# Neighbouring value blocks of a sparse-attention tile: copied on chip from the preceding tile's buffer instead of loaded

## The chip, the cores and the metric

The kernel runs on one core of a Trainium2 chip. The core has a matrix engine (PE, with its weight loads as PEld), a vector engine (DVE), a scalar engine (ACT), a general engine (Pool, or GpSimd), and SP, which issues most of the DMA transfers. SBUF, the on-chip memory, has 128 partitions; PSUM, in banks, takes what PE writes. Each engine works through its own queue in order and waits on semaphores for the others.

The metric is the device time of one execution in microseconds. The profile and the trace come from one execution taken by the hardware profiler; times inside it count from the span's start.

## The reference: what is computed

Block-sparse attention, then a mixture of experts that sends every token to one expert. Cut to what matters:

```python
B, H, S, D = 4, 8, 768, 64      # block = 32, so 24 blocks of 32 rows
scores = q @ k^T / sqrt(D)
mask = |blk_i - blk_j| <= 1                                  # the row's own block and its two neighbours
mask |= blk_i == 0 or blk_j == 0 or blk_i == 23 or blk_j == 23   # first and last block: dense
mask |= three sampled blocks per row block
attn = softmax(where(mask, scores, -1e9)) @ v
x = attn as (3072 tokens, 512)
e = argmax(x @ w_gate + modality_bias[modality_id])
out = gate * (relu(x @ w1[e]) @ w2[e])                       # 8 experts, 512 -> 1024 -> 512
```

The change touches only the values `v` that the sparse rows of the attention read.

## The kernel before

**Tiles.** The batch is cut into two halves of two sequences (`half`). In a half, the first and last row block are dense work (items `"d"`), and the other 22 row blocks are taken in pairs: tile `m` (0 to 10) holds row blocks `i = 2m+1` and `i+1`. There are 22 such sparse tiles, numbered `g = 11 * half + m`. Each row block (`n` = 0 or 1) attends to eight blocks: four that both row blocks of the tile share (`i`, the first block, the last block, `i+1`) and four of its own (one outer neighbour, `i-1` or `i+2`, and three sampled).

**Value buffers.** Two buffers `vbuf` are used in turn, by `g % 2`. Each has 128 partitions and three columns of 1024 values (two sequences of 512). A block takes 32 partitions of one column:

| partitions | column 0 (own blocks of `n` = 0) | column 1 (shared) | column 2 (own blocks of `n` = 1) |
|---|---|---|---|
| 0 to 31 | sampled | block `i` | block `i+2` |
| 32 to 63 | sampled | first block | sampled |
| 64 to 95 | sampled | last block | sampled |
| 96 to 127 | block `i-1` | block `i+1` | sampled |

`fetch_v` (line 472) fills the fixed places: the first and last block once per buffer and half (line 478, only for `m < 2`), `i` and `i+2` by one load (line 479), `i-1` and `i+1` by another (line 480). `fetch_own` (line 484) loads the six sampled blocks, whose numbers are read into registers on SP, by six loads (line 492). `weigh_shared` (L551) multiplies column 1, `weigh_own` (L560) columns 0 and 2. Keys have buffers of their own, `kbuf`, which Pool fills from dense keys already on chip (`share_k`, L454, L458 and, for the sampled blocks, L469).

**Order.** The order of the instructions on each engine is written out by hand. The work is a list of items (a dense pair of heads, or one row block of one sequence of a sparse tile, so four items a sparse tile). A loop over ticks `t` runs each stage of the items with a lag in ticks after the item's own number (`LAG`, line 60): scores S 0, maximum M 1, exponential X 2, transposes T and copies A 4, the shared product W 5, the own product V 7, the division O 8. Inside a tick the stages come in the order `OTSMGVXAYW`, and side work is hooked between them at places 0 to 7. For the first 14 ticks the order is the token list `START` (line 50).

Side work is placed by ticks relative to `last(g)`, the number of the last item of tile `g`: the key sharing of tile `g` no earlier than three ticks before its first item (`QP`), `fetch_v` at `last(g-2) + 8`, place 2 (`VL`), which is right after the own product of the tile that used the buffer, and the two halves of `fetch_own` at `last(g-2) + 8` and `+ 10` (`VG`). SP issues all of these in order, with the loads of queries (L141), dense keys and values (L153, L159), the rows written to `x_d` (L322) and, towards the end of the attention, the first weights of the experts (L680, L684). At most a few DMA issues stand open at once; a further issue waits on SP.

Towards the end of the attention the first two expert groups are begun early (`early_groups`, one step a tick at place 2): weights are loaded, cast by ACT (L688) and split into a high and a low part by DVE or, for some pieces (`POOL_SPLITS`), by Pool (L689).

Of the kernel before, what the change touches and what calls it, by code (L numbers as in the profile page):

```python
# [15 lines left out]
ALU = mybir.AluOpType  # L16
# [4 lines left out]
P = 128  # L21
# [18 lines left out]
NM = NB // 2 - 1  # L40
# [12 lines left out]
O01 W02 tb tb T10 A03 tb X11 S13 A10 qp0 tb tb tb tb tb tb O02 M13 tb tb T11 tb tb  # L53
X12 kl1 S0000 S0001 A11 X13 tb h8 tb W03 T12 tb O03 M0000 tb M0001 W10 h9 tb A12 tb tb tb T13
A13 O10 tb qp1 S0010 X0000 W11 tb h10 M0010 X0001 tb vl0 v00 v10 X0010 S0011 S0100 tb tb h11 T0000 h12 tb
A0000 M0011 T0001 tb S0101 A0001 M0100 W12 W13 O11 v11 O12 O13 vl1 h13 X0011 v01
""".split()
START_TICKS = 14
DENSE_AFTER = (22, 38, 43, 45)
# [8 lines left out]
KL = (0, 3)  # L68
QP = (-3, 7)
VL = (8, 2)  # L70
VG = ((8, 4), (10, 6))

DENSE_IN = ((28, 32, 16, 24), (53, 53, 38, 46))
# [14 lines left out]
def attention_moe(ctx, tc, kD, qD, qH, v0, v1, blocks, modality, w_gate, bias, w1, w2, out):  # L88
    nc = tc.nc
# [27 lines left out]
    with ExitStack() as actx:  # L117
# [9 lines left out]
        def slot(n, dt=F32):  # L127
            return big.tile([P, 3 * 1024 + 2], dt, name="slot", tag=f"slot{n}", bufs=1)
# [7 lines left out]
        vbuf = [slot(7 + n)[:, 0:3072].rearrange("p (c f) -> p c f", c=3) for n in range(2)]  # L136
# [313 lines left out]
        def share_k(m, half):  # L450
            i, g = 2 * m + 1, half * NM + m
            kg = kbuf[g % 2]
            if m:
                nc.gpsimd.tensor_scalar(kg[:, 3:5, :], kbuf[(g - 1) % 2][:, 7:9, :], 1.0, 1.0, ALU.mult, ALU.mult)  # L454

            def put(slots, blocks):
                for b in range(HB):
                    nc.gpsimd.tensor_scalar(kg[:, slots, b * P:(b + 1) * P].rearrange("p s (c f) -> p c s f", c=2), kd[half * HB + b][:, :, blocks, :], 1.0, 1.0, ALU.mult, ALU.mult)  # L458

            if m < 2:  # L460
                put(slice(5, 7), slice(0, NB, NB - 1))
            if m == 0:
                put(slice(3, 5), slice(i - 1, i + 1))
            put(slice(7, 9), slice(i + 1, i + 3))
            _, regs = nc.values_load_multi_w_load_instructions(
                rb_i[0:1, 3 * i:3 * i + 6], [ET.Pool], min_val=0, max_val=NB - 1, skip_runtime_bounds_check_because=NO_CHECK)
            for k, reg in enumerate(regs):
                for b in range(HB):
                    nc.gpsimd.tensor_copy(kg[:, k + k // 3 * 6, b * P:(b + 1) * P].rearrange("p (c f) -> p c f", c=2), kd[half * HB + b][:, :, bass.ds(reg, 1), :].rearrange("p c j f -> p c (j f)"))  # L469


        def fetch_v(m, half):
            i, g = 2 * m + 1, half * NM + m
            vg = vbuf[g % 2]
            vrow = vH[half].rearrange("(j s) b f -> s j (b f)", s=BLK)
            if m < 2:
                for n, j in ((0, 0), (1, NB - 1)):
                    nc.sync.dma_start(vg[32 + 32 * n:64 + 32 * n, 1, :], vrow[:, j, :])
            nc.sync.dma_start(vg[0:32, 1:3, :], vrow[:, i:i + 3:2, :])
            nc.sync.dma_start(vg[96:P, 0:2, :], vrow[:, i - 1:i + 2:2, :])  # L480

        own = {}

        def fetch_own(m, half, n):
            i, g = 2 * m + 1, half * NM + m
            vg = vbuf[g % 2]
            vrow = vH[half].rearrange("(j s) b f -> s j (b f)", s=BLK)
            if g not in own:
                own[g] = nc.values_load_multi_w_load_instructions(
                    rb_i[0:1, 3 * i:3 * i + 6], [ET.SP], min_val=0, max_val=NB - 1, skip_runtime_bounds_check_because=NO_CHECK)[1]  # L490
            for k, reg in enumerate(own[g][3 * n:3 * n + 3]):
                nc.sync.dma_start(vg[32 * (k + n):32 * (k + n) + 32, 2 * n, :], vrow[:, bass.ds(reg, 1), :].rearrange("p j f -> p (j f)"))
# [612 lines left out]
        for k, it in enumerate(sparse[0] + sparse[1]):  # L1105
            items.append(it)
            if k in DENSE_AFTER:
                c = 2 * DENSE_AFTER.index(k)
# [5 lines left out]
        def side(t, f, place=7):  # L1114
            work_at.setdefault((t, place), []).append(f)
# [31 lines left out]
        def q_load(m, half):  # L1147
            qraw[m, half] = fetch_q(half, m)
# [7 lines left out]
        loads = {"blk": block_ids}  # L1156
        last = lambda g: at["s", g // NM, g % NM, 1, 1]
        for g in range(2 * NM):
            half, m = divmod(g, NM)
            t = at["s", half, m, 0, 0]  # L1160
            kl = lambda m=m, half=half: q_load(m, half)
            qp = lambda m=m, half=half: share_k(m, half)
            vl = lambda m=m, half=half: fetch_v(m, half)
            vg = [lambda m=m, half=half, n=n: fetch_own(m, half, n) for n in range(2)]
            if g < 2:
                loads.update({f"kl{g}": kl, f"qp{g}": qp, f"vl{g}": vl, **{f"v{n}{g}": vg[n] for n in range(2)}})
                continue
            kt = last(g - 2) + KL[0]
            pt = max(kt, t + QP[0])
            vt = last(g - 2) + VL[0]  # L1170
            side(kt, kl, KL[1])
            side(pt, qp, QP[1])
            side(vt, vl, VL[1])
            for n in range(2):
                side(last(g - 2) + VG[n][0], vg[n], VG[n][1])

# [162 lines left out]
```

## Time and profile before

| what | value |
|---|---|
| time, median of 3 runs | 562.62 us (561.59, 562.62, 565.06) |
| the profiled execution's own time | 561.07 us |
| its span in the trace | 559.4 us |
| mean granted PE clock | 0.983 of full speed |
| DMA bytes | 124.68 MB, 223 GB/s over the span |
| loads of 256 KB into value buffers and other slots, `slot<-v` | 44 |
| loads of 128 KB, `slot<-v` | 140 |

The span starts with loads and constants; the sparse tiles run from about 27 to 251 us, and the experts from there to 549 us, followed by the last writes.

How to read the lines: a row of the timeline has its start in microseconds, its length, the engine, the source line, the operation, the tiles as output<-input, the shape (partitions x elements), the count, and in brackets how long the engine stood idle before it and what ended that. `<-issue` means that the engine waited for nothing that the profile shows. A row of groups has the count, the busy time in microseconds, the mean of one in nanoseconds, and the idle time before it. A row of waits says who waited for whom: total, times, longest. A row of stretches has the stretch, its length, the busy time of PE, PEld, DVE, ACT and Pool with counts, the granted clock, the share of the DMA engines that was busy, and GB/s. A piece of the chain has start, length, engine and line. A row of one source line has minimum, median and maximum in nanoseconds.

### The profile page before, as it was taken

How to read it: one execution, taken by the hardware profiler on the slowest of the kernel's cores; microseconds unless marked ns; L12 is line 12 of the kernel's file. 1: busy time of each engine (PE TensorE's matmuls, PEld its weight loads, DVE VectorE, ACT ScalarE, POOL GpSimd, SP SyncE). 2: the span in 40 equal slices, each digit the busy share in tenths (PEclk: the TensorE clock that was granted, in tenths of full speed). 3: DMA queues.
4: the chain of work that ended last, by engine and by line, in shares of the span. 5: the costliest groups of instructions: out<-in, count | busy, mean ns of one | idle time of the engine just before them, and what ended most of it. 6: DMA issues, size and time to landing. Idle time of an engine off the chain costs nothing.

```text
span 559.4 us, 18870 instructions
## 1 busy us (share of the span) xinstructions
PE 519.3 (93%) x7274; PEld 434.7 (78%) x7274; DVE 368.9 (66%) x1151; ACT 327.1 (58%) x746; POOL 180.2 (32%) x413
## 2 busy tenths in 40 slices
PE   7799888899999996989999999999999999999992
PEld 5477656667776774779888898989989899898972
DVE  4796666677687885985986456655566555665560
ACT  3679755776777874762564545545455454554560
POOL 1746524533354553403134330320303213032130
PEclk9999998999999997999999999999999999999997
DMA  7885999797977789977567875757667567675730
GB/s 288 291 245 151 258 237 256 209 247 234 234 148 214 211 219 262 253 200 264 190 244 242 322 242 192 263 187 240 236 199 260 189 223 243 206 259 185 237 111 22
DMA packets 48691, 124.68 MB, mean 223 GB/s; under 512 B 7376, under 2 KB 7504, under 8 KB 48592
## 3 DMA queue, kind: packets, MB, share of 16 engines
q1 hardware_dynamic: 44512, 110.26, 65.9%
q0 software_dynamic: 4080, 13.12, 6.6%
q8 instruction: 59, 0.97, 0.7%
q14 instruction: 40, 0.33, 0.2%
HBM read 110.76 MB, written 12.86 MB: 221 GB/s over the span
## 4 chain that ended last, share of the span: by engine, by line
PE 76%; DMA 10%; DVE 4%; issue 4%; ACT 2%; SPq 1%; POOL 1%; POOLq 0%; ACTq 0%; DVEq 0%
PE bank L504 8%; PE bank L729 8%; PE bank L712 7%; PE bank L728 7%; PE bank L727 7%; PE bank L714 7%; PE bank L713 7%; PE bank L529 7%; DMA slot<-v 6%; PE bank L551 3%; PE bank L560 3%; PE bank L577 2%; DMA slot<-w 2%; DMA x_d<-xr 2%; PE bank L701 2%
## 5 line engine op out<-in xcount | busy, mean ns | idle before, releaser
L689 DVE TENSOR_TENSOR slot<-slot 128x1024 fp32r<-128x1024 f32 x96 | 120.2, 1257 | 100.6 <-ACT slot L688 95.9
L688 ACT CAST slot<-slot 128x1024 fp32r<-128x1024 f32 x104 | 108.0, 1049 | 107.0 <-PE bank L729 46.6
L712 PE MATMUL bank<-slot 128*128 128x256 f32 x384 | 108.4, 282 | 0.0
L714 PE MATMUL bank<-slot 128*128 128x256 f32 x384 | 107.7, 281 | 0.0
L713 PE MATMUL bank<-slot 128*128 128x256 f32 x384 | 107.6, 280 | 0.0
L520 ACT ACTIVATE a<-y,mn 128x256 f32<-128x256 f32 x176 | 87.9, 506 | 6.7 <-DVE mn L512 6.2
L729 PE MATMUL bank<-slot 128*128 128x512 f32 x200 | 79.2, 396 | 1.1 <-DVE slot L720 1.1
L738 POOL DMA_INDIRECT out<-slot,si x21 | 21.2, 1009 | 182.4 <-ACT slot L734 179.4
L727 PE MATMUL bank<-slot 128*128 128x512 f32 x200 | 80.0, 400 | 0.0
L728 PE MATMUL bank<-slot 128*128 128x512 f32 x200 | 79.0, 395 | 0.0
L469 POOL COPY slot<-slot 128x128 f32 x264 | 64.6, 297 | 27.6 <-issue 27.5
L712 PEld LDWEIGHTS bank<-slot 128*128 128x128 f32 x384 | 72.2, 188 | 0.6
L713 PEld LDWEIGHTS bank<-slot 128*128 128x128 f32 x384 | 72.2, 188 | 0.4
L714 PEld LDWEIGHTS bank<-slot 128*128 128x128 f32 x384 | 72.2, 188 | 0.0
L512 DVE CUSTOM_DVE_ANT_1 y<-bank,smask 128x256 f32<-128x256 f32 x176 | 66.1, 417 | 1.9 <-PE bank L504 1.6
L529 PE MATMUL bank<-ident,a 128*128 128x128 f32 x352 | 55.1, 286 | 7.2 <-DVE mn L512 5.4
L534 ACT COPY at<-bank 128x512 f32<-128x512 f32 x66 | 38.0, 577 | 29.4 <-PE bank L529 28.8
L504 PE MATMUL bank<-slot,q_raw 64*32 64x256 f32 x1408 | 52.4, 393 | 1.6 <-DVE mn L512 1.0
L529 PEld LDWEIGHTS bank<-ident,a 128*128 128x128 f32 x352 | 39.0, 144 | 14.0 <-DVE mn L512 5.0
L729 PEld LDWEIGHTS bank<-slot 128*128 128x128 f32 x200 | 37.6, 188 | 11.0 <-DVE slot L720 2.0
L728 PEld LDWEIGHTS bank<-slot 128*128 128x128 f32 x200 | 37.6, 188 | 8.1 <-DVE slot L689 0.4
L727 PEld LDWEIGHTS bank<-slot 128*128 128x128 f32 x200 | 37.6, 188 | 7.8 <-ACT slot L887 0.3
(290 smaller groups left out, 804.0 us busy)
## 6 DMA issues: line engine op xcount, KB each, us to landing
slot<-w SPq DMA_DIRECT2D x105, 512.0 KB
slot<-v SPq DMA_DIRECT2D x140, 128.0 KB
slot<-v SPq DMA_DIRECT2D x44, 256.0 KB
slot<-v SPq DMA_DIRECT2D x8, 768.0 KB
x_d<-xr SPq DMA_DIRECT2D x22, 256.5 KB
q_raw<-qH SPq DMA_DIRECT2D x22, 256.0 KB
slot<-kD SPq DMA_DIRECT2D x7, 768.0 KB
x_d<-xrd SPq DMA_DIRECT2D x2, 256.5 KB
```

The source lines that it names most:

```text
L504: nc.tensor.matmul(sp[u][32 * pr:32 * pr + 32, b * 256:(b + 1) * 256], lhsT=q[r, b * NPAIR + pr, n, :], rhs=kv[r, s0:s0 + 8, b, pr, :], st ...
L512: nc.vector.tensor_tensor_reduce(y[:, u, :].rearrange("p (s f) -> p s f", s=8), sp[u][:, b * 256:(b + 1) * 256].rearrange("p (s f) -> p s ...
L520: nc.scalar.activation(a[:, u, :], y[:, u, :], AF.Exp, bias=mn[:, u:u + 1], scale=-1.0, accum_out=total[:, u:u + 1])
L529: nc.tensor.transpose(tp[:, k:k + P], a[:, u, c * P:(c + 1) * P], ident)
L688: nc.scalar.copy(h, staged(n))
L689: (eng or (nc.gpsimd if n in POOL_SPLITS else nc.vector)).tensor_tensor(l, staged(n), h.bitcast(F32), ALU.subtract)
L712: nc.tensor.matmul(o, lhsT=h[:, fs], rhs=xh[g % 2][:, c, :], start=c == 0 and f % 2 == 0, stop=False)
L713: nc.tensor.matmul(o, lhsT=h[:, fs], rhs=xl[g % 2][:, c, :], start=False, stop=False)
L714: nc.tensor.matmul(o, lhsT=l[:, fs], rhs=xh[g % 2][:, c, :], start=False, stop=c == 3 and f % 2 == 1)
L727: nc.tensor.matmul(o, lhsT=hh[0][:, f, ts_], rhs=h[:, fs], start=f == 0, stop=False)
L728: nc.tensor.matmul(o, lhsT=hh[0][:, f, ts_], rhs=l[:, fs], start=False, stop=False)
L729: nc.tensor.matmul(o, lhsT=hl[f // 4][:, f % 4, ts_], rhs=h[:, fs], start=False, stop=f == 7)
```

## The change

For every tile but the first of a half, two of the four blocks that `fetch_v` loaded are no longer loaded. Block `i-1` of tile `m` is block `i+1` of tile `m-1`, and block `i` of tile `m` is block `i+2` of tile `m-1`; both lie in the other buffer, in the same partitions, one column to the right. Pool copies them with two operations of 32 partitions by 1024 elements (`share_v`). The two loads stay, with one block each. The first tile of a half loads all four as before.

The copies of tile `g` are placed at `last(g-2) + 11`, place 2 (`VS`), three ticks after the tile's loads; those of tile 1 are a token of `START`. They read the buffer of tile `g-1` and write the buffer that tile `g-2` has left. So they must follow the own product of tile `g-2` and the loads of tile `g-1`; the shared product of tile `g`, and the loads of tile `g+1` into the places that were read, must follow them.

```diff
-A0000 M0011 T0001 tb S0101 A0001 M0100 W12 W13 O11 v11 O12 O13 vl1 h13 X0011 v01
+A0000 M0011 T0001 tb S0101 A0001 M0100 W12 W13 O11 v11 O12 O13 vl1 vs1 h13 X0011 v01
...
 VL = (8, 2)
+VS = (11, 2)
...
-            nc.sync.dma_start(vg[0:32, 1:3, :], vrow[:, i:i + 3:2, :])
-            nc.sync.dma_start(vg[96:P, 0:2, :], vrow[:, i - 1:i + 2:2, :])
+            if m == 0:
+                nc.sync.dma_start(vg[0:32, 1:3, :], vrow[:, i:i + 3:2, :])
+                nc.sync.dma_start(vg[96:P, 0:2, :], vrow[:, i - 1:i + 2:2, :])
+                return
+            nc.sync.dma_start(vg[0:32, 2, :], vrow[:, i + 2, :])
+            nc.sync.dma_start(vg[96:P, 1, :], vrow[:, i + 1, :])
+
+
+        def share_v(m, half):
+            g = half * NM + m
+            new, old = vbuf[g % 2], vbuf[(g - 1) % 2]
+            for r, c in ((slice(96, P), 0), (slice(0, 32), 1)):
+                nc.gpsimd.tensor_scalar(new[r, c, :], old[r, c + 1, :], 1.0, 1.0, ALU.mult, ALU.mult)
...
             side(vt, vl, VL[1])
+            if m:
+                side(last(g - 2) + VS[0], lambda m=m, half=half: share_v(m, half), VS[1])
```

More of the change, by code (lines that the diff above doesn't have):

```diff
@@ L1165, in attention_moe @@
             if g < 2:
-                loads.update({f"kl{g}": kl, f"qp{g}": qp, f"vl{g}": vl, **{f"v{n}{g}": vg[n] for n in range(2)}})
+                loads.update({f"kl{g}": kl, f"qp{g}": qp, f"vl{g}": vl, "vs1": lambda: share_v(1, 0), **{f"v{n}{g}": vg[n] for n in range(2)}})
                 continue
```

## The prediction

> **What bounds the kernel now.** I read the page first: busy shares, the slices, and the chain that ended last.
>
> ```profile
> PE 519.3 (93%) x7274; PEld 434.7 (78%) x7274; DVE 368.9 (66%) x1151; ACT 327.1 (58%) x746; POOL 180.2 (32%) x413
> PEclk9999998999999997999999999999999999999997
> DMA  7885999797977789977567875757667567675730
> PE 76%; DMA 10%; DVE 4%; issue 4%; ACT 2%; SPq 1%; POOL 1%; POOLq 0%; ACTq 0%; DVEq 0%
> ```
>
> TensorE (PE) is busy for 93% of the span and carries 76% of the chain. DMA carries 10%, and its busiest slices lie in the first half, which is the attention. So the next view is the busy time by stretch: all of the steady attention, its last part, and the experts.
>
> ```profile
> core 0: us, PE busy (x) PEld busy (x) DVE busy (x) ACT busy (x) POOL busy (x), PEclk, DMA share, GB/s
> 40.00:251.00 211.00, 190.56 (x4790) 145.69 (x4790) 154.30 (x761) 151.55 (x485) 92.00 (x295) 0.97 0.87 224
> 206.00:250.00 44.00, 36.28 (x862) 28.71 (x862) 33.85 (x179) 28.18 (x83) 15.93 (x32) 0.88 0.96 244
> 251.00:549.00 298.00, 296.88 (x1966) 266.23 (x1955) 186.17 (x262) 151.87 (x190) 71.14 (x56) 1.00 0.65 222
> ```
>
> In the experts PE idles 1.1 us of 298, so whatever the change wins or loses up to 251 us moves the end by the same amount, and nothing in the experts can be won by it. In the attention PE idles 20.4 us of 211, of which 7.7 us in 206 to 250, where DMA is 96% busy. Only this idle time, and the low clock there, can be won. Which of it is due to DMA, PE's waits in 40 to 251 us tell, and then its timeline:
>
> ```profile
> PE bank L529 <- DVE mn L512: 5.4, 2, 4.9
> PE bank L560 <- DMA slot<-v: 3.0, 3, 1.4
> ```
>
> ```profile
> 80.64 1.09 PE L560 MATMUL bank<-slot,at 128*32 128x64 f32 x62 [1.45 <-DMA slot<-v]
> 217.55 1.12 PE L529 MATMUL bank<-ident,a 128*128 128x128 f32 x4 [4.92 <-DVE mn L512]
> 244.12 1.09 PE L560 MATMUL bank<-slot,at 128*32 128x64 f32 x62 [0.95 <-DMA slot<-v]
> 250.14 1.09 PE L560 MATMUL bank<-slot,at 128*32 128x64 f32 x62 [0.59 <-DMA slot<-v]
> ```
>
> Three waits of 1.45, 0.95 and 0.59 us are for the sampled blocks of values (L492). The longest, 4.92 us, names VectorE (DVE), but DVE was itself held up. ScalarE (ACT) and the DMA issues just before show by what:
>
> ```profile
> 214.85 1.04 ACT L688 CAST slot<-slot 128x1024 fp32r<-128x1024 f32 x1 [4.45 <-issue]
> 206.47 1.74 SPq L479 DMA_DIRECT2D slot<-v  x1
> 208.26 0.42 SPq L480 DMA_DIRECT2D slot<-v  x1
> 209.58 0.92 SPq L680 DMA_DIRECT2D slot<-w  x2
> ```
>
> ACT stands 4.45 us before a cast that reads the first expert weights, whose load was issued at 209.58, 5.27 us before. The exponentials queue behind that cast, and so do PE's transposes. Right in front of the weights in the DMA queue stand the two loads that the change halves.
>
> **The change, part by part.** *Removed.* A block is 32 x 1024 x 4 = 131,072 bytes. For 20 of the 22 tiles each of the two loads carries one block in place of two: 262,144 bytes less a tile, 5.24 MB in all. At the 244 GB/s of 206 to 250 us that is 1.07 us of the queue for each tile. The number of DMA issues on SP stays at two a tile, so SP's own time does not change. Where the queue has a backlog, what stands behind a tile's pair can land up to 1.07 us earlier; where it has none, nothing is won. Term by term:
> - A, the wait at 80.64: one pair (tile 4) stands ahead in the same backlog. Bounds 0 and -1.45, taken -1.0, since 1.07 is less than the wait.
> - B, the stall before 217.55: the pair at 206.47 and 208.26 stands directly before the weights. Bounds 0 and -2.1 (two tiles' worth), taken -1.0.
> - C, the low clock after that stall, shown below: bounds 0 and -4.2, taken -1.0, because the stall gets shorter but stays.
> - D, the waits of 0.95 and 0.59 at the end: two more pairs stand ahead. Bounds 0 and -1.54; taken -1.0, since PE will arrive there earlier too.
>
> *Added on Pool (GpSimd).* Two copies a tile, 32 partitions by 1024 elements each, on an engine that had no such shape.
>
> ```profile
> L458 POOL TENSOR_SCALAR slot<-slot 128x256 f32<-128x256 f32 x50 | 20.1, 405 | 9.8 <-DMA slot<-kD 5.4 <-PE bank L504 2.4
> L454 POOL TENSOR_SCALAR slot<-slot 128x512 f32<-128x512 f32 x20 | 12.4, 621 | 67.7 <-PE bank L544 35.1 <-PE bank L504 29.2 <-PE bank L426 3.5
> ```
>
> The same operation takes 405 ns at 256 elements and 621 ns at 512: 0.84 ns an element and some 190 ns fixed. My estimate for 1024 is 1.05 us, 2.10 us a tile, 42 us in all. No row has fewer than 128 partitions at this width, so the bounds are 0.62 us (the 512 row, if fewer partitions were cheaper) and 2.39 us (a two-input operation of 1024, row below). I take 1.05, the same operation carried on. [...]
>
> Does Pool have room? One tile of its steady work:
>
> ```profile
> 171.56 0.62 POOL L454 TENSOR_SCALAR slot<-slot 128x512 f32<-128x512 f32 x1 [2.82 <-PE bank L504]
> 172.14 0.89 POOL L458 TENSOR_SCALAR slot<-slot 128x256 f32<-128x256 f32 x2
> 174.17 2.95 POOL L469 COPY slot<-slot 128x128 f32 x12 [1.14 <-issue]
> 179.33 0.62 POOL L454 TENSOR_SCALAR slot<-slot 128x512 f32<-128x512 f32 x1 [2.21 <-PE bank L544]
> ```
>
> The sharing of keys for tile 16 takes 171.56 to 177.12, then Pool idles 2.21 us until the next. By the order of the ticks the copies for tile 14 fall into this gap: 177.12 to 179.22. They just fit. Their inputs are there by then, as the source tile was loaded a whole tile before. Queued behind them is the key sharing of tile 17, which would start at 179.33 anyway. Who waits for them:
>
> ```profile
> 181.58 0.34 SPq L479 DMA_DIRECT2D slot<-v  x1
> 184.32 0.98 PE bank L551 x32
> ```
>
> The next load into the source buffer (tile 15) is issued at 181.58, 2.4 us after the copies; PE's shared product of tile 14 starts at 184.32, 5.1 us after. Both have room, so I cost the order at nothing here. If that room goes, SP stands, and behind it all loads of sampled blocks. It is thinnest for tile 20, where the copies come behind a weight split on Pool:
>
> ```profile
> 233.83 2.39 POOL L689 TENSOR_TENSOR slot<-slot 128x1024 fp32r<-128x1024 f32 x1
> 238.71 0.31 PE L551 MATMUL bank<-slot,at 128*64 128x64 f32 x2
> ```
>
> The split ends at 236.22, the copies at 238.32, the product begins at 238.71. Term F: bounds 0 and +2, taken +0.3.
>
> *Added for DVE.* Pool's operations hold up some of DVE's:
>
> ```profile
> 233.96 2.29 DVE L303 TENSOR_TENSOR oh<-desc,first 128x16 bf16<-128x16 f32 x1
> L303 DVE TENSOR_TENSOR oh<-desc,first x12: 167/174/2291, 58.5 to 263.7; 128x16 bf16<-128x16 f32 x12
> 20.59 0.62 POOL L454 TENSOR_SCALAR slot<-slot 128x512 f32<-128x512 f32 x1
> 20.65 0.56 DVE L415 TENSOR_TENSOR su<-sm 128x1 f32<-128x1 f32 x1
> L538 DVE TENSOR_TENSOR rexp<-sums,quad 128x32 f32<-128x32 f32 x22 | 5.4, 244 | 0.0
> L363 DVE TENSOR_SCALAR lhs<-iota_f,rlo,code 128x128 f16<-128x128 f32 x19 | 7.0, 366 | 0.0
> L415 DVE TENSOR_TENSOR su<-sm 128x1 f32<-128x1 f32 x14 | 2.6, 191 | 0.0
> L314 DVE TENSOR_SCALAR gs<-gs 128x2 f32<-128x2 f32 x11 | 2.4, 215 | 0.3
> ```
>
> L303 takes 174 ns, but 2291 when it starts under the split of 233.83 to 236.22: it ends with it. L415 at 20.65 ends with the key copy of 20.59. Both read only SBUF. The groups shown with such operands count 22 + 19 + 14 + 11 + 12 = 78 instructions in the attention. The copies fill 42 us of 231, 18%, so some 14 would meet one and wait 0.53 us on average (half a copy): 7.5 us of DVE waits. DVE idles a quarter of the attention, and softmax stages lie one or more ticks of 1.9 us apart, so most is hidden. Term E: bounds 0 and +7.5, taken +0.7.
>
> Sum: -1.0 - 1.0 - 1.0 - 1.0 + 0.7 + 0.3 = -3.0 us. The profiled execution took 561.07 us and would become 558.1; it lies 0.3% under the median of the runs, 562.62. Applied to that median: 559.6.
>
> **The rivals.** *Nothing comes of it.* The loads were mostly hidden: PE's waits that name them come to 3.0 us. What makes them late may be the sampled blocks themselves and the weights, which stay. With A to D halved and E and F doubled the sum is zero: 562.6.
>
> *The low clock goes as well.* The stretches of 3.41 us around the long stall:
>
> ```profile
> 212.33:215.75 3.42, 0.30 (x12) 0.21 (x9) 0.00 (x0) 0.90 (x1) 2.26 (x9) 1.00 0.99 341
> 215.75:219.16 3.41, 1.61 (x12) 1.55 (x13) 3.10 (x9) 2.69 (x10) 2.03 (x5) 0.50 1.06 228
> 219.16:222.57 3.41, 3.41 (x54) 1.86 (x53) 2.08 (x12) 2.69 (x10) 0.00 (x0) 0.50 1.04 241
> 222.57:225.99 3.42, 3.42 (x42) 3.30 (x41) 3.26 (x27) 0.52 (x1) 0.00 (x0) 0.50 1.04 222
> ```
>
> After 0.30 us of PE work in the first, the granted clock is 0.50 for the next three. From 217.55 to 225.99 PE works at half speed, which costs half of 8.44 us, 4.2 us. A stall short enough to spare that gives -2.0 for the other terms and -4.2: 556.4. Against it: the stall has to fall far below 4.92 - 1.0 us. [...]
>
> *Slower: DVE takes the place of DMA.* If the waits of E fall on softmax steps that PE is about to need, all 7.5 us count: 562.62 - 3.7 + 7.5 = 566.4. For it: 233.96 shows 2.1 us lost at once. Against it: one copy holds DVE for 1.05 us at most, less than a tick. It decides from where PE loses more than the 3.7 us that the other terms give, half of the 7.5.
>
> **How the numbers follow.** Forecast (557.6 to 561.6) 0.46; nothing 0.18; clock spared 0.20; DVE or Pool in the way 0.16 (Pool too, since copies at the bound of 2.39 us would make its tile 5.56 + 4.78 = 10.3 us against an interval of 7.77). The predicted time is 559.6. The range, 555.5 to 566.0, takes in the clock case and the milder half of the DVE case and leaves out some 0.17. A measurement of this kernel can tell about 1% from no change, that is below 557.0 or above 568.2: faster 0.20 (most of the clock case, a tail of the forecast), slower 0.09 (the far end of the last case), within 1% 0.71.
>
> **What would show it.** Right: DMA bytes down to 119.4 MB; a new Pool group of 40 copies near 1.05 us; PE's waits for value loads near 1 us in place of 3.0; the stall before the first weight cast near 3.9 us. Wrong: copies over 1.5 us, Pool waits in front of PE's scores, SP's value loads waiting for Pool, DVE's two-input operations stretched with PE's waits for `mn` growing, or the stall unchanged, which would mean that the weights' own transfer sets it.

## The result, and the profile after

| | before | changed |
|---|---|---|
| first comparison: median (lowest to highest) | 562.71 us (561.59 to 565.06, 4 runs) | 554.69 us (553.29 to 557.68, 4 runs) |
| second comparison, another chip | 562.52 us (558.66 to 568.69, 19 runs) | 557.51 us (553.32 to 558.96, 8 runs) |
| ratio and 95% interval, first | | 0.9885 [0.9841, 0.9930] |
| ratio and 95% interval, second | | 0.9921 [0.9890, 0.9952] |

The ratios leave out runs more than 1.5% above the fastest of their kernel and are not the quotients of the medians in the table, which are 0.9857 and 0.9911. The change makes the kernel about 1% faster. The first median is 0.8 us under the low end of the forecast range, the second inside it.

The page of the changed kernel (its profiled execution took 553.29 us and was the fastest of the four): the busy line, the granted clock and DMA by slices, the chain, and the new group of copies.

```profile
PE 517.9 (94%) x7274; PEld 433.7 (79%) x7274; DVE 381.4 (69%) x1151; ACT 327.5 (59%) x746; POOL 221.6 (40%) x453
PEclk9999999999999997999999999999999999999997
DMA  8983898866945689847767875757667566675830
DMA packets 47411, 119.43 MB, mean 217 GB/s; under 512 B 7376, under 2 KB 7504, under 8 KB 47312
PE 76%; DVE 8%; DMA 6%; issue 4%; POOL 2%; SPq 1%; ACT 1%; POOLq 0%; DVEq 0%
L492 POOL TENSOR_SCALAR slot<-slot 32x1024 f32<-32x1024 f32 x40 | 41.7, 1043 | 12.7 <-DMA slot<-x_d,gi_e 3.6
```

Pool has 41.4 us more work, of which the copies are 41.7. DVE has 12.5 us more, though its instruction count is the same. DMA's share of the chain falls from 10% to 6%, and that of DVE rises from 4% to 8%. The same kernel by stretches (columns as in the prediction's view of stretches):

```profile
40.00:246.00 206.00, 188.37 (x4793) 143.95 (x4792) 167.61 (x762) 151.96 (x485) 131.46 (x334) 0.98 0.74 203
246.00:544.00 298.00, 296.48 (x1949) 265.69 (x1947) 184.53 (x261) 152.06 (x190) 70.66 (x56) 1.00 0.66 222
```

In the attention DMA is 74% busy in place of 87%. The experts take the same 298 us. The span fell by 7.85 us, from 559.36 to 551.51: the first expert matmul starts at 245.52 instead of 251.16 (-5.64), the stretch from there to the last matmul takes 298.05 instead of 298.07, and the rest, after the last matmul, takes 7.94 instead of 10.13 (-2.19). PE's long waits towards the end of the attention are these (timeline of PE in the changed kernel):

```profile
206.17 0.55 PE L1010 MATMUL bank<-hoh,lhs 128*128 128x2 f16 x16 [0.80 <-DVE hoh L1000]
210.70 1.12 PE L541 MATMUL bank<-ident,a 128*128 128x128 f32 x4 [3.98 <-DVE mn L524]
227.78 0.65 PE L579 MATMUL bank<-ident,xr 128*128 128x128 f32 x4 [1.38 <-DVE mn L524]
244.50 1.09 PE L572 MATMUL bank<-slot,at 128*32 128x64 f32 x62 [1.46 <-DMA slot<-v]
```

The stall that was 4.92 us is 3.98. Of the two last waits for values (0.95 and 0.59) one is left, of 1.46 us.

**The 2.2 us after the last matmul.** What SP waited for in the last 25 us or so, first before, then changed (who waited for whom: total, times, longest):

```profile
SPq L1335 <- PEq L1335: 4.6, 2, 4.1
```

```profile
SPq L1349 <- PEq L1349: 2.4, 2, 1.9
```

The view names PE's queue, but the records of the sequencers show another engine. Before, Pool's last branch ends 7.78 us ahead of the span's end and the drain that follows it begins 2.62 us later; in the changed kernel that gap is 0.43 us. Over the profiles of this study the gap belongs to the program: 0.43 in ten profiles of kernels with 417 to 453 instructions on Pool (two of the changed kernel, and two each of two variants, among them), 2.62 to 2.71 in the three kernels with 413, 413 and 493, and 0.12 in one with 455. Before, two transfers of 8 KB on the instruction queue q14 run inside the gap (552.58 to 553.24 us), and the drain begins 0.96 us after the second; in the changed kernel the gap holds none, and two such transfers begin 0.56 us after the drain does. A wait of Pool for its own instructions would look like this; that cause is argued, not shown. What is shown is where the 2.2 us lie, and that neither the copies nor the halved loads decide them: three kernels with the halved loads and all copies have 0.43 (the changed kernel), 2.65 (every copy twice) and 2.71 (all copies on ACT). The three kernels that were profiled twice have the short gap both times; each kernel with the long one was profiled once.

### The profile page after: what moved, and what is told of

The parts are those of the page before. It is cut to its first block, busy times and chain, and to the rows that moved or that the text cites. A ratio compares the mean times of both kernels' runs of the same rounds, so it can differ in the third digit from the quotient of the medians.

```text
span 551.5 us, 18915 instructions
## 1 busy us (share of the span) xinstructions
PE 517.9 (94%) x7274; PEld 433.7 (79%) x7274; DVE 381.4 (69%) x1151; ACT 327.5 (59%) x746; POOL 221.6 (40%) x453
## 4 chain that ended last, share of the span: by engine, by line
PE 76%; DVE 8%; DMA 6%; issue 4%; POOL 2%; SPq 1%; ACT 1%; POOLq 0%; DVEq 0%
PE bank L741 8%; PE bank L724 8%; PE bank L740 8%; PE bank L739 8%; PE bank L725 8%; PE bank L726 8%; PE bank L516 7%; PE bank L541 6%; DMA slot<-v 4%; PE bank L563 3%; PE bank L572 3%; PE bank L713 2%; PE bank L589 2%; PE bank L429 2%; DVE y L524 1%
## 5 line engine op out<-in xcount | busy, mean ns | idle before, releaser
L726 PE MATMUL bank<-slot 128*128 128x256 f32 x384 | 107.7, 281 | 0.0
L741 PE MATMUL bank<-slot 128*128 128x512 f32 x200 | 79.2, 396 | 1.1 <-DVE slot L732 1.1
L740 PE MATMUL bank<-slot 128*128 128x512 f32 x200 | 79.1, 395 | 0.0
L724 PEld LDWEIGHTS bank<-slot 128*128 128x128 f32 x384 | 72.2, 188 | 0.6
L725 PEld LDWEIGHTS bank<-slot 128*128 128x128 f32 x384 | 72.1, 188 | 0.5
L726 PEld LDWEIGHTS bank<-slot 128*128 128x128 f32 x384 | 72.2, 188 | 0.0
L516 PE MATMUL bank<-slot,q_raw 64*32 64x256 f32 x1408 | 50.8, 387 | 0.7 <-DVE mn L524 0.4
L492 POOL TENSOR_SCALAR slot<-slot 32x1024 f32<-32x1024 f32 x40 | 41.7, 1043 | 12.7 <-DMA slot<-x_d,gi_e 3.6
L741 PEld LDWEIGHTS bank<-slot 128*128 128x128 f32 x200 | 37.6, 188 | 11.0 <-DVE slot L732 2.0
L740 PEld LDWEIGHTS bank<-slot 128*128 128x128 f32 x200 | 37.6, 188 | 8.1 <-DVE slot L701 0.4
```

The costliest lines, as they stand in the source:

```text
L516: nc.tensor.matmul(sp[u][32 * pr:32 * pr + 32, b * 256:(b + 1) * 256], lhsT=q[r, b * NPAIR + pr, n, :], rhs=kv[r, s0:s0 + 8, b, pr, :], st ...
L724: nc.tensor.matmul(o, lhsT=h[:, fs], rhs=xh[g % 2][:, c, :], start=c == 0 and f % 2 == 0, stop=False)
L725: nc.tensor.matmul(o, lhsT=h[:, fs], rhs=xl[g % 2][:, c, :], start=False, stop=False)
L726: nc.tensor.matmul(o, lhsT=l[:, fs], rhs=xh[g % 2][:, c, :], start=False, stop=c == 3 and f % 2 == 1)
L740: nc.tensor.matmul(o, lhsT=hh[0][:, f, ts_], rhs=l[:, fs], start=False, stop=False)
L741: nc.tensor.matmul(o, lhsT=hl[f // 4][:, f % 4, ts_], rhs=h[:, fs], start=False, stop=f == 7)
```

## The experiments

Four theories were set against each other. They are called Theory A to D, to tell them from the terms A to F of the prediction. *Theory A*: the smaller volume is worth more than its waits for values, since it also shortens other waits, and the copies are nearly free. *Theory B*: only some 3 us of waits for values are won, the rest is chance. *Theory C*: the copies cost several microseconds, and the volume is worth correspondingly more. *Theory D*: the loads were hidden anyway.

Totals of different variants also hold the 2.2 us, so the attention was cut in two as well. "First half" runs from the ninth group of 32 score matmuls (54.68 us before) to the shared product of tile 12 (166.44 us before), "second half" from there to the first expert matmul (251.16 us before). The second half is divided once more, at the shared product of tile 17 (207.44 us before): five tiles of steady work stand ahead of it, and behind it the first expert groups are begun beside the attention. The cuts come from one profile in each row.

| kernel | ratio to before [95%] | first half, us | second half, us | of it tiles 12 to 17 | of it from tile 17 on | after the last matmul, us |
|---|---|---|---|---|---|---|
| before | 1 | 111.8 | 84.7 | 41.0 | 43.7 | 10.1 |
| changed | 0.9885 [0.9841, 0.9930] | 106.2 | 85.0 | 39.3 | 45.7 | 7.9 |
| changed, again | 0.9921 [0.9890, 0.9952] | 110.5 | 85.3 | 39.0 | 46.3 | 7.9 |
| copies three ticks earlier | 0.9899 [0.9868, 0.9929] | 107.8 | 86.3 | 39.4 | 46.9 | 7.9 |
| shared in the first half only | 0.9846 [0.9791, 0.9901] | 106.0 | 86.7 | 42.6 | 44.1 | 7.9 |
| the same, again | 0.9857 [0.9825, 0.9890] | 108.5 | 87.2 | 42.8 | 44.4 | 7.9 |
| shared in the second half only | 0.9940 [0.9905, 0.9976] | 112.1 | 85.4 | 39.4 | 46.0 | 7.9 |
| last three tiles loaded | 0.9844 [0.9809, 0.9879] | 110.9 | 85.2 | 43.5 | 41.7 | 7.9 |
| copies of the second half on ACT | 0.9891 [0.9860, 0.9923] | 107.0 | 83.7 | 42.8 | 40.9 | 7.9 |
| all copies on ACT | 0.9934 [0.9904, 0.9963] | 111.5 | 83.4 | 41.6 | 41.8 | 10.2 |
| every copy twice | 1.0099 [1.0062, 1.0135] | 110.0 | 95.3 | 46.8 | 48.5 | 10.2 |
| half the loads, no copies | not comparable | 107.0 | 79.0 | 39.5 | 39.5 | not comparable |
| the same, again | not comparable | 113.6 | 79.2 | 39.5 | 39.8 | not comparable |
| quarter of the loads, copies | not comparable | 107.7 | 84.7 | 39.3 | 45.4 | not comparable |

How far one profile may be trusted is in the table itself. The kernel that shares only in the second half does nothing new in the first, and yet its profile stood 1.9 us behind before at 77 us and level with it at 166 us. The first half of the changed kernel took 106.2 us once and 110.5 once. The second half repeats better: 85.0 and 85.3, 86.7 and 87.2, 79.0 and 79.2. Still, the second half of the kernel that shares only in the first is the program of before there, and took 86.7 and 87.2 where before took 84.7.

### The changed kernel once more

> The changed kernel once more, as it stands, so that the experiments beside it have it on the same chip. Theory A (the gain is the smaller DMA volume; it shows in PE's waits for value blocks, in PE's waits for its own instructions, which come over the same DMA engines, and in fewer stretches of low clock): 554 to 557 us. Theory B (only the value waits of some 3 us are won, and the rest of the 8 us was luck of one profile and four runs): 557 to 560 us.

Measured: 557.51 us, 0.9921 of before. The gain is there again, smaller. The waits for values are in other places in this profile (timeline of PE):

```profile
69.27 1.09 PE L572 MATMUL bank<-slot,at 128*32 128x64 f32 x62 [1.59 <-DMA slot<-v]
79.78 1.09 PE L572 MATMUL bank<-slot,at 128*32 128x64 f32 x62 [1.42 <-DMA slot<-v]
239.03 1.15 PE L563 MATMUL bank<-slot,at 128*64 128x64 f32 x32 [3.04 <-POOL slot L492]
```

The wait of tile 4, 1.45 us before and absent in the first profile of the changed kernel, is 1.42 here, and tile 3 waits 1.59. At the end PE waits 3.04 us for the copies of tile 20 themselves. So "the wait is gone" cannot be read from one profile.

The expectation also names waits of PE for its own instructions. The page of before has an instruction queue, q8, on the same 16 DMA engines (59 packets, 0.97 MB). From 40 to 251 us before, PE has eleven waits that name no releaser, 7.5 us in all and 1.63 at most; ten of them end 1.2 to 1.7 us after a packet of 16 KB on q8 has ended, the eleventh 0.5 us after. In the changed kernel, from 40 to 246 us, there are nine, 3.6 us in all, and five end 1.2 to 1.5 us after such a packet. That these waits are for instructions is inferred from that alone.

### Half the loads, no copies

```diff
-            if m:
+            if False:
                 side(last(g - 2) + VS[0], lambda m=m, half=half: share_v(m, half), VS[1])
```

Tile 1 and tile 12 also load all four blocks, so that every place is written once. The shared block `i` and the block `i-1` of all later tiles are left as an earlier tile loaded them, so the outputs are others, tokens go to other experts and the time of the experts is not comparable.

> The loads are halved as in the change, but the copies on Pool are left out: from the third tile of a half on, two of the four neighbouring blocks keep old values. What is left of the change is its smaller volume alone. Theory A (volume is the gain, copies are nearly free): 1 to 2 us under the changed kernel, 553 to 555. Rival C (the copies cost several us through waits of DVE and late Pool work, and the volume is worth more than is seen): 4 us or more under the changed kernel, 550 or less. Theory B: as the changed kernel, within 1 us, and not more than 4 us under the kernel before.

> Half the loads and no copies, once more (values of the two blocks are those of another tile, so tokens go to other experts and the time after the attention is not comparable). The first expert matmul started at 239.2 us in its first profile, 251.2 in before, 245.5, 250.5 and 248.6 with one set of copies, 259.9 with two. Theory C (the copies cost 8 to 10 us and the halved loads are worth some 12): 238 to 241 again. Theory A (the copies cost 1 us): 245 or later.

Measured: the first expert matmul starts at 239.2 us in the first profile and at 247.0 in the second. The second refutes what Theory C expected of that one number and lies where Theory A had it; the first half differs by 6.5 us between the two profiles of one kernel. The second half, though, takes 79.0 and 79.2 us, 6 us less than in all four profiles of kernels that share there on Pool (85.0 to 86.3). By its two parts, all of this lies from tile 17 on: 39.5 and 39.8 us without copies, 45.7 to 46.9 with them. Tiles 12 to 17 take 39.5 and 39.5 without and 39.0 to 39.4 with them, so there one set of copies costs PE nothing. The early work of the experts, whose tokens are others in this kernel, falls into the part that differs. Waits of PE in the second half, second profile:

```profile
PE bank L541 <- DVE mn L524: 3.0, 1, 3.0
PE bank L572 <- DMA slot<-v: 1.2, 2, 0.8
PE bank L572 <- issue: 1.0, 2, 0.5
```

### A quarter of the loads, copies kept

```diff
-            nc.sync.dma_start(vg[0:32, 2, :], vrow[:, i + 2, :])
-            nc.sync.dma_start(vg[96:P, 1, :], vrow[:, i + 1, :])
+            nc.sync.dma_start(vg[0:32, 2, 0:512], vrow[:, i + 2, 0:512])
+            nc.sync.dma_start(vg[96:P, 1, 0:512], vrow[:, i + 1, 0:512])
```

The second sequence's values of two blocks a tile are left out here, so routing and the experts' time differ as above. The edit also lets tiles 1 and 12 load what the copies bring, which holds PE up for 4.70 us at 40.64; the total is not used.

> As the changed kernel, copies included, but each of the two remaining loads of a tile (from the third tile of a half on) brings only half of its columns, so that the volume falls by as much again per load: another 2.4 MB of 119.4; the other columns keep old values. Theory A: the waits go on shrinking with the volume, 1 to 3 us under the changed kernel, and PE's idle time that names no releaser falls further. Rival D (the change took what there was, and the loads are hidden now): the changed kernel within 1 us.

Measured: the second half takes 84.7 us. With the copies in place, halving the two loads again changes nothing there (84.7 against 85.0 to 86.3), while taking the copies away changes it by 6 us. By parts it is the same: 39.3 and 45.4 us, like the changed kernel. In one profile, then, the copies and not what is left of the volume set the length of the second half, and they do it from tile 17 on.

### The copies three ticks earlier

`VS = (8, 2)` in place of `(11, 2)`.

> The changed kernel with the copies placed at tick +8 in place of +11, directly behind the tile's loads and ahead of the next key sharing and of the weight splits on Pool. In the changed kernel's trace the copies of tile 20 stand until 231.0 us for the gather of expert rows, SP stands behind them with the loads of tile 21, and PE waits 1.46 us for those at 243 us. Theory A: that wait goes, 1 to 2 us under the changed kernel. Rival: the copies now hold up the first weight split or the key sharing instead; no gain, or 1 to 2 us slower.

Measured: 556.07 us against 557.51 of the changed kernel beside it; the intervals of the ratios overlap almost wholly. Where the copies stand among these ticks makes no difference that this measurement tells. The wait of 1.46 us that Theory A expected to go is 1.0 us here.

### Every copy twice

```diff
-            for r, c in ((slice(96, P), 0), (slice(0, 32), 1)):
+            for r, c in ((slice(96, P), 0), (slice(0, 32), 1)) * 2:
```

> The changed kernel, with each of the two copies of a tile issued twice, one behind the other (80 copies in place of 40; the second pair writes the same values again). Loads are those of the changed kernel. The changed kernel itself has had medians of 554.7 and 557.5 us; 556.5 is taken for it. Theory A (the copies are nearly free, +1.0 us for all 40 as forecast by the terms E and F): another +1 to +2 us, 557.5 to 558.5. Theory C (the copies give back 5 us or more, by VectorE's operations that are stretched under them and by their place behind the weights' split on Pool): another 5 us or more, 561.5 to 566. In both, the copies' busy time on Pool goes from 41.7 to 83 us.

Measured: 569.63 us, 1.0099 of before. That is 10 to 12 us over the changed kernel by the ratios, of which 2.2 us lie after the last matmul. Theory A expected 1 to 2, Theory C 5 or more, and the time lies above the range that either gave. The first half took no longer than others (110.0 us); the second took 95.3, some ten more, of which 7.5 in tiles 12 to 17. Pool's timeline shows why. First the changed kernel, two tiles of its steady work and the start of the next:

```profile
188.44 2.16 POOL L492 TENSOR_SCALAR slot<-slot 32x1024 f32<-32x1024 f32 x2
190.57 0.61 POOL L455 TENSOR_SCALAR slot<-slot 128x512 f32<-128x512 f32 x1
191.15 0.88 POOL L459 TENSOR_SCALAR slot<-slot 128x256 f32<-128x256 f32 x2
193.17 2.92 POOL L470 COPY slot<-slot 128x128 f32 x12 [1.14 <-issue]
196.17 2.16 POOL L492 TENSOR_SCALAR slot<-slot 32x1024 f32<-32x1024 f32 x2
...
203.91 2.16 POOL L492 TENSOR_SCALAR slot<-slot 32x1024 f32<-32x1024 f32 x2
```

Then the kernel with every copy twice:

```profile
196.88 4.40 POOL L492 TENSOR_SCALAR slot<-slot 32x1024 f32<-32x1024 f32 x4
201.25 0.61 POOL L455 TENSOR_SCALAR slot<-slot 128x512 f32<-128x512 f32 x1
201.83 0.88 POOL L459 TENSOR_SCALAR slot<-slot 128x256 f32<-128x256 f32 x2
203.85 2.88 POOL L470 COPY slot<-slot 128x128 f32 x12 [1.14 <-issue]
206.82 4.60 POOL L492 TENSOR_SCALAR slot<-slot 32x1024 f32<-32x1024 f32 x4
...
217.02 5.25 POOL L492 TENSOR_SCALAR slot<-slot 32x1024 f32<-32x1024 f32 x4
...
227.82 4.40 POOL L492 TENSOR_SCALAR slot<-slot 32x1024 f32<-32x1024 f32 x4
```

In the changed kernel a tile takes Pool 7.73 us (196.17 - 188.44, and 203.91 - 196.17 gives 7.74) without a gap that has a releaser. Pool is full. PE's own tiles, by the starts of its shared products in the same profile, take 7.34, 7.17, 7.79 and 7.17 us:

```profile
170.37 1.13 PE L563 MATMUL bank<-slot,at 128*64 128x64 f32 x32
177.71 1.13 PE L563 MATMUL bank<-slot,at 128*64 128x64 f32 x32
184.88 1.13 PE L563 MATMUL bank<-slot,at 128*64 128x64 f32 x32
192.67 1.13 PE L563 MATMUL bank<-slot,at 128*64 128x64 f32 x32
199.84 1.13 PE L563 MATMUL bank<-slot,at 128*64 128x64 f32 x32
```

So Pool falls behind PE: the next key sharing (206.04) begins 6.2 us after the shared product of tile 17, where it was 3.85 before. PE does not pay for that in these tiles. None of its waits in them names Pool, and they take less time than before, 39.3 us against 41.0. With the copies doubled a tile takes Pool 9.94, 10.20 and 10.80 us, 7.7 us more for the three than at 7.73 each. Pool sets the pace, and PE waits for the copies directly (its timeline):

```profile
191.39 1.15 PE L563 MATMUL bank<-slot,at 128*64 128x64 f32 x32 [2.21 <-POOL slot L492]
201.33 1.98 PE L563 MATMUL bank<-slot,at 128*64 128x64 f32 x32 [2.43 <-POOL slot L492]
```

In the first half dense work lies between the tiles: before the change, the shared products of tiles 4 and 12 start at 74.90 and 166.44 us, 11.4 us a tile. There Pool has more room, which fits the 110.0 us.

### Sharing in one half only

```diff
-            if m == 0:
+            if m == 0 or not (half * NM + m < 11):
...
-            if m:
+            if m and g < 11:
```

The other variant has `> 11` in both places.

> Blocks are shared only for the 10 tiles of the first half of the tiles (1 to 10); the 10 tiles of the second half load all four blocks as before the change. The forecast's terms give: A (-1.0) stays, E halves (+0.35), B, C and F (the stall at 217.55, the low clock after it, the copies of tile 20) fall away, D stays half: some -1.0 us against 562.6, 561.6. Theory A (the gain is the smaller volume anywhere, by shorter waits of TensorE for its own instructions and fewer stretches of low clock): about half to two thirds of the -6 us or more, since by the profiles -7 us had come by 118 us: 557 to 559.

> The kernel that shares blocks only for tiles 1 to 10, once more, beside the two new versions. It measured 556.99 us, 0.9846 of before [0.9791, 0.9901]. If sharing in the second half is worth nothing, it is again at or under the changed kernel: 0.983 to 0.989. If the first figure was chance, half of the changed kernel's gain: 0.994 to 0.996.

> Blocks are shared only for the 10 tiles of the second half (12 to 21); tiles 1 to 10 load all four blocks as before the change. The forecast's terms give: B, C, D and F stay, A falls away, E halves: -1.0 -1.0 -1.0 +0.35 +0.3, some -2.3 us against 562.6, 560.3. Theory A (volume): a third to a half of -6 us, 559.5 to 561. Theory C (copies dear in the second half, where Pool and VectorE also split and gather for the experts): no gain or a loss, 562 to 564, and then the kernel that shares only in the first half is the best.

Measured: shared in the first half only, 556.99 us (0.9846), and in the repetition 556.53 (0.9857); in the second half only, 560.52 (0.9940). Less the 2.2 us after the last matmul, which all three have, and with 562.6 us for before, these are -6.5, -5.9 and -1.2 us for the attention; the changed kernel gives -4.3 and -2.2 by the same working. So nearly all comes from the first half, and sharing in the second half adds nothing that shows, or takes something back. Whether it takes something back stays open: the intervals overlap or touch, and the changed kernel did not run beside these. The first-half-only kernel came out at the low end of Theory A's 557 to 559, and faster than the 561.6 of the forecast's terms. For the second half alone, Theory A's range and the forecast's terms take in the 560.52; Theory C's 562 to 564 lies 1.5 us above it, less than the 2.2 us after the last matmul, which no theory had. The profiles agree on the first half: the nine of kernels that share there with copies on Pool have 106.0 to 110.9 us, the two with all loads 111.8 and 112.1. They do not show which waits went, and the kernel without copies had 107.0 once and 113.6 once.

### The last three tiles loaded

The condition is `g < 19` in both places: tiles 19 to 21 load all four blocks.

> As the changed kernel, but tiles 19, 20 and 21 load all four blocks again (shared: tiles 1 to 10 and 12 to 18, 17 of 20). Theory F (a large part of what the copies give back is made by the last tiles, whose copies stand on Pool among the split of the experts' first weights and the gathers of the expert rows): against before, the changed kernel loses 2.0 to 2.9 us between the first value matmul of tile 19 and the first expert matmul in every profile (the kernel that shares only in the first half 0.8), so 1.2 to 2 us come back: 554.5 to 555.5 where the changed kernel is 556.5. Rival (the copies cost about the same everywhere): 3 of 20 pairs of copies give 3/20 of some 9 us, 1.3 us, and 3/20 of the loads cost as much as that or more: 556 to 557.5.

Measured: 556.08 us, 0.9844, the lowest ratio of all. Its interval [0.9809, 0.9879] lies under that of the changed kernel's second comparison and overlaps the first. The profile carries only half of the reason that was expected. From tile 17 on it took 41.7 us in place of 45.7 to 46.9. But tiles 12 to 17, where the two kernels are alike, took 43.5 in place of 39.0 to 39.4, so its second half is as long as the changed kernel's, 85.2 us. Whether the last copies or a Pool that had caught up in the slower tiles made the last part short stays open. That this version beats the changed kernel is likely and not shown.

### The copies on ACT

```diff
-                nc.gpsimd.tensor_scalar(new[r, c, :], old[r, c + 1, :], 1.0, 1.0, ALU.mult, ALU.mult)
+                nc.scalar.copy(new[r, c, :], old[r, c + 1, :])
```

> The same two copies of a tile at the same places, on ScalarE in place of Pool (ScalarE is busy for 59% of the span, Pool for 40%). Theory A (copies on Pool nearly free): no gain from moving them, and some loss, since ScalarE's evictions and exponentials of the scores stand behind them: 556.5 to 562. Theory C (Pool's copies hold VectorE's operations and wait behind the weights' split): VectorE's busy time falls from 381 back to some 370 us, and the time falls by several us where ScalarE has the room: 551 to 555.

> As the changed kernel, with the copies of tiles 1 to 10 on Pool and those of tiles 12 to 21 on ScalarE. Theory C (on Pool the copies of the second half cost what the loads gain): by the profiles the stretch from tile 12's first value matmul to the first expert matmul stands against before at +0.2, +0.5 and +1.6 us in the three with the copies on Pool, and at -1.4 with them on ScalarE, so 1.5 to 3 us less than the changed kernel, 553.5 to 555. Rival (what is between those profiles is chance): 556 to 557.5.

The second of the two has this edit for tiles 12 to 21 only. Measured: 559.99 us (0.9934) with all copies on ACT, 557.34 (0.9891) with those of the second half. The former has the long 10.2 us after the last matmul; with that set aside both are level with the changed kernel, as Theory A and the rival of the second run had it. The attention by stretches, first the changed kernel's second profile, then all copies on ACT:

```profile
40.00:251.00 211.00, 192.74 (x4795) 148.29 (x4796) 164.16 (x763) 152.24 (x485) 131.04 (x333) 0.95 0.72 201
```

```profile
40.00:251.00 211.00, 193.80 (x4792) 145.89 (x4791) 154.52 (x755) 187.17 (x527) 91.88 (x295) 0.97 0.72 199
```

DVE's busy time is 164.16 us with the copies on Pool and 154.52 with them on ACT; before it was 154.30. So the ten microseconds of DVE are time under Pool's copies and nothing else. Taking them away did not make the kernel faster by an amount that shows: the stretching of DVE is real and mostly hidden. The second half took 83.4 and 83.7 us with the copies on ACT, 1.3 to 2.9 us less than on Pool, and still some 4.4 us more than without copies: ACT pays for them too, with 1044 ns each ahead of the exponentials, and it pays elsewhere: tiles 12 to 17 take 41.6 and 42.8 us (39.0 to 39.4 with the copies on Pool), the part from tile 17 on 41.8 and 40.9 (45.7 to 46.9).

None of the four theories holds throughout. Theory A fits the first half and tiles 12 to 17, where the copies cost nothing that shows. Theory C fits the part from tile 17 on. Theory B's 3 us are too little and Theory D's hidden loads wrong for the kernel that shares only in the first half, whose two ratios lie well under 1.

## Why the prediction was right, and where it was not

The forecast was -3.0 us, all of it in the attention. By the ratios the whole gain was 6.5 us and then 4.4 us, by the medians 8.0 and 5.0; less the 2.2 us at the end, the attention gave 4.3 and 2.2, or 5.8 and 2.8. The sum was right within what can be measured. That is in part luck: its parts were not right, and their errors, of opposite signs, partly cancelled.

- **"Whatever the change wins or loses up to 251 us moves the end by the same amount."** For the experts this holds to 0.02 us. It failed behind them: the last 10.13 us became 7.94. That is the part of the first median's distance from the forecast that is settled, and the forecast did not look behind the experts.
- **A, the wait of tile 4 (-1.0).** Not confirmed as a wait: it was 0 in one profile of the changed kernel and 1.42 in the other. What first-half sharing is worth is larger than A: 6 us by the runs of the kernel that shares only there (-6.5 and -5.9). The term was undersized, because the volume was given credit only for the waits that name the value loads. Which other waits went, differs from profile to profile, so it stays open.
- **B and C, the stall at 217.55 and the low clock (-1.0 each).** The stall is 3.98 and 2.87 us in the two profiles of the changed kernel, so B has the right sign; but it is 3.9 and 4.4 in the two of the kernel that does not share there, against 4.92, so most of it is no more than scatter. For C nothing is shown: the low clock around that stall lasts 6.8 us in one profile of the changed kernel (stall 3.98) and 10.2 in the other (2.87), 10.2 before.
- **D, the waits at the end (-1.0).** Did not come: 1.46 us is left of 1.54.
- **B to F together are the step that failed most, twice over.** In the second half the copies were priced at no more than +0.7 (E, for the whole attention) and, for tile 20, +0.3 (F), and the volume at -3.0. The runs show some +6 us for the copies (79.1 without, 85.0 to 86.3 with them on Pool) and some -5.6 us for the volume (84.7 before, 79.1): both terms are too small, some six and two times, with opposite signs. The 6 us lie from tile 17 on; of the 5.6, 1.5 lie in tiles 12 to 17. Two reservations belong to this. The kernel without copies sends tokens to other experts, and their early work falls into that last part; but the kernels with the copies on ACT, which send every token where before sends it, take 3.9 to 6.0 us less there too than those with the copies on Pool. And the unchanged second half of the kernel that shares only in the first took 86.7 and 87.2 us, so the worth of the volume is uncertain by some 2.5 us. The ten microseconds from one set of copies to two are another cost: 7.5 of them lie in tiles 12 to 17, where the first set costs nothing.
- **The room on Pool.** "They just fit", said the prediction of the gap of 2.21 us, and costed the order at nothing. The copies took 1043 ns against 1.05 forecast and 41.7 us against 42. But the room was read from one interval of 7.77 us. From 171.56 to 211.28 the same view of before has intervals from 7.18 to 8.68, and ahead of one of them a gap in which two copies do not fit:

```profile
195.19 0.62 POOL L454 TENSOR_SCALAR slot<-slot 128x512 f32<-128x512 f32 x1 [0.93 <-PE bank L544]
```

  So Pool, at 7.73 us a tile, ran late, and through tile 17 this cost PE nothing. It may be what costs from there on. The prediction had named the danger ("If that room goes, SP stands"): in the five profiles with one set of copies on Pool throughout the second half (the quarter of the loads among them), SP issues the first expert weights 2.4 to 3.8 us after the start of tile 17's shared product and their first cast on ACT begins 7.55 to 8.18 us after it (timelines of SP and ACT); without copies it is -0.3 and 1.0, and 4.6 and 5.5. That the late Pool is the cause is argued, not shown, since before, with all its loads, has 2.1 and 7.4. The 10.3 us that the prediction gave for copies twice as dear is what the doubled copies showed: 9.94 to 10.80.
- **F.** The copies of tile 20 were expected right behind the second split of weights. They began 3.64 us after it had ended:

```profile
224.99 2.37 POOL L701 TENSOR_TENSOR slot<-slot 128x1024 fp32r<-128x1024 f32 x1
231.00 4.53 POOL L492 TENSOR_SCALAR slot<-slot 32x1024 f32<-32x1024 f32 x4 [3.64 <-DMA slot<-x_d,gi_e]
```

  This row puts the wait down to the gathers of the expert rows, that of the changed kernel's second profile (3.48 us) to a load of weights; which of them the copies have to wait for, and why, stays open. The prediction had asked only what stands ahead of the copies on Pool, not what they would wait for themselves. It costs PE 3.04 us in the second profile and nothing at that place in the first.
- **The rivals.** *Nothing comes of it* fits the second half alone. *The low clock is spared* came nearest in time (556.4), by a mechanism that did not happen: the mean granted clock of the profiled run is 0.985 after 0.983, and 0.976 in the second profile. *DVE in the way* named a real effect and its order of size (7.5 us forecast, 10 to 12.5 measured), and the runs with the copies on ACT show that most of it is hidden.

## What to carry to other kernels

Moving traffic from DMA to an engine is worth what that engine has left, stage by stage, and one interval does not tell what it has left: look at the shortest, not at one. Here one set of copies cost the bounding engine nothing in the steady tiles, although Pool needed 7.73 us for a tile that PE often did in 7.17; the price came behind them, where Pool, SP and ACT also begin the experts. Ask of an added instruction both what stands ahead of it on its engine and what it must itself wait for. Doubling a cost tells where an engine runs out of room, and this it told in one comparison; it does not tell what the single cost is, since the second set of copies lost 7.5 us in tiles in which the first lost nothing. And cut a stage into parts before giving a cause for its length: several microseconds of scatter between two profiles of one kernel hide it in the total.

## What the runs showed of the hardware

- A copy of 32 partitions by 1024 elements took as long as the rows for 128 partitions (405 ns at 256 elements, 621 at 512) led one to expect, 1.05 us: 1043 ns on Pool; on ACT it took 1044 ns. On Pool, two copies to different partitions ran one behind the other, 2.16 us a pair.
- Two small DVE operations under Pool's copies took 1.02 and 0.95 us. In the changed kernel, beside the copies that run from 203.91 to 206.07:

```profile
203.96 1.02 DVE L315 TENSOR_SCALAR gs<-gs 128x2 f32<-128x2 f32 x1
205.15 0.95 DVE L1000 CAST hoh<-ho 128x32 f16<-128x32 f32 x1
L315 DVE TENSOR_SCALAR gs<-gs x12: 160/169/1019, 58.3 to 260.8; 128x2 f32<-128x2 f32 x12
```

  The median of L315 is 169 ns; the other operation of L1000, 128x36, took 174 ns.
- From its last branch to its final drain Pool took 0.43 us in ten profiles, 2.62 to 2.71 in three and 0.12 in one; three kernels that were profiled twice had the same 0.43 both times.
